# Who makes the rests of the weights: GpSimd or VectorE, and how many tiles are made ahead

## The chip, the cores and the metric

The kernel runs on one core of a Trainium2 chip. The time is device microseconds (us) of one execution; the median of three runs of the kernel before is 943.08 us (942.50 to 943.26). Lower is better.

## The reference

Windowed attention, then an MLP with the maximum of three products, then a gated MLP, all in float32:

```python
scores = 1/sqrt(64) * q @ k.T + bias          # 4 batches, 8 heads, 576 tokens, 64 deep
attn   = softmax(where((0 <= i - j) & (i - j < 128), scores, -1e9))
x      = (attn @ v)                           # 2304 tokens x 512
h      = maximum(maximum(x @ w1, x @ w2), x @ w3)      # w: 512 x 768
x      = h @ w_out                                      # 768 x 512
g      = x @ w_gate; val = x @ w_val                    # 512 x 1536
out    = (g * sigmoid(g) * val) @ w_out2                # 1536 x 512
```

The weights of both MLPs are float64 in memory.

## The kernel before

TensorE multiplies float32 here as three products of a narrower format: an operand is split into its rounding (the head) and what is left (the rest), and head x head + head x rest + rest x head is summed in PSUM (`mm3`). So every operand needs a rounding and a subtraction, `low`, which makes the rest.

A weight tile (128 rows x 512 columns) comes from memory as pairs of 32-bit words. `prep_w` makes a float32 of it and splits it: ScalarE scales the upper word (L93), VectorE does three bit steps (L94, L95, L97), ScalarE rounds to the head (L100), and GpSimd subtracts the head, which is the rest (L80, called at L101). In the rows these are `wf` (the work tile, two places), `wr` (the raw words) and `w`, `wo` or `u` (the made tile of the first MLP's up or down weights, or of the second MLP).

The first MLP runs per sub-chunk of a batch, 256 or 320 tokens, eight in all, with the attention of the sub-chunks to come between its products; its 18 up tiles and 6 down tiles (in 12 halves) are made while the first sub-chunks run. For each 128 features VectorE takes the maximum of three products (L155), and GpSimd rounds and splits it (`h`). The result y goes to memory.

The second MLP runs over all 2304 tokens in chunks of 512 (the last has 256), with its 36 tiles resident: for each of 12 blocks f of 128 features the gate's, the value's and the output's. `gate(c, f)` multiplies y by two tiles (24 products), ScalarE takes the sigmoid (L503), VectorE multiplies twice (L504, L505), GpSimd rounds (L83) and splits (L80) the result `a`; `down(c, t, f)` adds it to the output sums of 128 tokens (3 products each). A gate stands ahead of the down products of the block before it. `load_y(0)` loads and splits the four pieces of y of the first chunk through the two `wf` places. Raw words of the second MLP have four places (`RAWS`).

C2 and C3 say how many of the 36 tiles are made at which point: `conv[:C2]` are spread among the last sub-chunk's up products (and the down products ahead of them), `conv[C2:C3]` with `load_y(0)` among its last down products, three more ahead of gate(0, 0), and then three for each block of chunk 0. The order of the instructions of each engine is set from this program order by a scheduler that models the engines' times; each engine then runs its own list strictly in order. All loads and stores are issued by SyncE (SP), also in order.

Of the kernel before, what the change touches and what calls it, by code (L numbers as in the profile page):

```python
# [30 lines left out]
FILL = -float(2.0 ** 100)  # L31
# places for the second MLP's words to arrive
RAWS = 4
NATIVE = 12, 10
C0, C1, C2, C3 = 0, 0, 6, 9
HIGH, EARLY = 100, 3
# [11 lines left out]
LN, LT, LV = 1, 2, 4  # L48
# the upper word of a float64 of 2**-127, read as a float32
LEAST = 1.0 * 2.0 ** -15  # L50
# [3 lines left out]
def kernel(ctx: ExitStack, tc, qk0, qk1, vv, w123, wo1, wgv, wo2, out):  # L54
    """Windowed attention, then max-of-three MLP, then gated MLP, all in float32.

    Products of float32 operands run as three float32r passes: an operand is split exactly into a
    12-bit head (its rounding to float32r) and the 12-bit rest, and head*head + head*rest +
    rest*head is summed in PSUM. Weights come as the words of float64 and become float32 here.

    The first MLP runs per sub-chunk of a batch (256 and 320 tokens), with the attention of the
    sub-chunks to come between its products; the second runs over all tokens with its weights
    resident, in chunks of 512.
    """
    nc = tc.nc
# [18 lines left out]

    # -------- weights: [P, head/rest, 512] tiles
    def prep_w(raw, t):
        """float64 words to float32 to head and rest. The bits: sign and top exponent bit, the
        exponent's low seven bits and the mantissa's first twenty, then its next three; under
        2**-126 it becomes 0."""
        n = raw.shape[1]  # L90
        lo, hi = raw[:, :, 0], raw[:, :, 1]
        w = wraw.tile([P, 512], I32, tag="wf", name="wf")[:, :n]
        nc.scalar.activation(out=w.bitcast(F32), in_=hi.bitcast(F32), func=AF.Copy, scale=2.0 ** -112)  # L93
        nc.vector.tensor_scalar(out=w, in0=w, scalar1=3, scalar2=None, op0=ALU.logical_shift_left)  # L94
        nc.vector.scalar_tensor_tensor(out=w, in0=hi, scalar=-0x80000000, in1=w,  # L95
                                       op0=ALU.bitwise_and, op1=ALU.bitwise_or)
        nc.vector.scalar_tensor_tensor(out=lo, in0=lo, scalar=29, in1=w,  # L97
                                       op0=ALU.logical_shift_right, op1=ALU.bitwise_or)
        lo = lo.bitcast(F32)
        nc.scalar.copy(t[:, 0], lo)  # L100
        low(nc.gpsimd, t[:, 1], lo, t[:, 0])  # L101

# [6 lines left out]
    def mm3(ps, wt, col, xt_h, xt_l, first, last):  # L109
        """ps += w.T @ x over one 128-deep slice, w's columns col..col+128."""  # L110
        wh, wl = wt[:, 0, col:col + P], wt[:, 1, col:col + P]
        nc.tensor.matmul(ps, wh, xt_h, start=first, stop=False)  # L112
        nc.tensor.matmul(ps, wh, xt_l, start=False, stop=False)  # L113
        nc.tensor.matmul(ps, wl, xt_h, start=False, stop=last)  # L114

    # -------- first MLP
    x_t, w1, wo, hs = {}, {}, {}, {}
# [9 lines left out]
    def prep_up(f, e):  # L127
        if (f, e) not in w1:
            load_up(f, e)
        raw, w1[f, e] = w1[f, e], up_tile(f"w1_{f}_{e}")  # L130
        prep_w(raw, w1[f, e])

    def prep_down(k):
        wo[k] = down_tile(f"wo_{k}")
        for i in range(2):
            src = wo1[k * P:(k + 1) * P, i * 256:i * 256 + 256]
            raw = words(src, wraw, "wr", 256) if i else words(src, tmp, "y", 256)
            prep_w(raw, wo[k][:, :, i * 256:i * 256 + 256])

    def up_groups(b, s):  # L140
        """The up products of a sub-chunk, three experts per 128 features."""
        n = SUBS[s][1]
# [21 lines left out]
    def down_groups(b, s):  # L164
# [8 lines left out]
        def group(ds):  # L173
            # the last features of two columns after the others of both
            ps = [ps_m.tile([P, 512], F32, tag="m", name="ps2") for d in ds]
# [28 lines left out]

    # -------- attention pieces
    def load_pair(b, s, p):
# [30 lines left out]
    def native(b, s, p, i):  # L237
        """Whether the scores (0) or the values (1) are multiplied in float32 itself, which takes
        the tensor engine longer and the others less: at the start, while it has no other work."""
        return SKIP[i] <= todo.index((b, s, p)) < NATIVE[i]  # L240
# [18 lines left out]
    class Unit:  # L259
        """A pair of heads and a block of 128 queries, against the block's keys and those before."""  # L260

# [9 lines left out]
    def st_scores(u):  # L271
# [5 lines left out]
        for a in range(2):  # L277
# [8 lines left out]
            nc.tensor.matmul(o, q, kl[:, c0 - nq:c1 - nq], start=False, stop=True)  # L286
        # query q sees key k of its own block for k <= q, of the block before for k > q: one square
        own = sc[:m, :, P:]
# [30 lines left out]
    def st_transpose(u):  # L319
        """The weights with keys in front, head and rest, of the block before and of the own block."""  # L320
        m = u.mq
# [75 lines left out]

    # attention in the order of its pieces: a unit's later pieces come after the next units' first
    units = [Unit(b, s, p, j) for b, s in order for p in range(NP) for j in BLOCKS[s]]
# [45 lines left out]
    def spread(main, *others, early=0):  # L445
        """Calls main's pieces in turn, with each other list's spread evenly in front of all but
        the last few."""
        done = [0] * len(others)
        for i, g in enumerate(main):
            for n, o in enumerate(others):  # L450
                while done[n] < len(o) and done[n] * (len(main) - early) <= i * len(o):
                    o[done[n]]()
                    done[n] += 1
            g()
        for n, o in enumerate(others):
            for piece in o[done[n]:]:
                piece()

    # -------- second MLP
    w2 = {}  # L460

    def second(w2pool, raws2, ps_o):
        y_t, acts, ps = {}, {}, {}

        def prep(f, i):
# [6 lines left out]
            src = wgv[f, :, i] if i < 2 else wo2[f * P:(f + 1) * P]  # L472
            prep_w(words(src, raws2, "wr2", 512), t)

# [16 lines left out]
        def gate(c, f):  # L491
            """128 features of the gated product."""
            n = CHUNKS[c][1]
# [18 lines left out]
        def down(c, t, f):  # L512
            """What those features give 128 tokens."""
            if f == 0:
# [13 lines left out]

    # the tensor engine's clock rises after some microseconds of work
    cold = tmp.tile([P, 512], BF16, tag="m0", name="cold")  # L530
# [36 lines left out]

    # the products of a feature block go into the outputs of the whole chunk while the next
    # block's run; the first chunk goes over each weight as it comes
    spread([lambda: gate(0, 0)], conv[C3:C3 + 3])  # L570
# [53 lines left out]
```

## Time and profile before

| | |
|---|---|
| median of three runs | 943.08 us |
| span of the profiled execution | 939.2 us (some 3.9 us lie around it) |
| TensorE (PE) busy | 904.2 us, 96% of the span |
| VectorE (DVE) busy | 497.4 us, 53% |
| GpSimd (POOL) busy | 472.4 us, 50% |
| ScalarE (ACT) busy | 354.2 us, 38% |
| chain that ended last | PE 76%, DVE 11%, issue 4%, POOL 4%, DMA 4% |

Shares of the whole span hide the stages: the attention and the first up products to about 125 us, the rest of the first MLP to 463 us, the first chunk of the second MLP with the making of its weights to 560 us, and four more chunks to 935 us. "PEclk" in a row is the mean clock that TensorE was granted in that stretch, as a share of full speed (1.0 is 2.4 GHz, 0.5 is 1.2 GHz).

### The profile page before, as it was taken

The numbers are of one execution on the slowest core, as the hardware profiler recorded it, in microseconds if no ns is written. First come the engines' busy times: TensorE is split into PE (matmuls) and PEld (weight loads), VectorE is DVE, ScalarE is ACT, GpSimd is POOL, SyncE is SP. The second block draws the span as 40 slices with busy tenths as digits, with TensorE's granted clock in tenths as the row PEclk, the third lists the DMA queues.
The fourth block names the chain that finished last, engine by engine and source line by source line (L and its number), as shares of the span: only waits on it lengthen the run. The fifth ranks groups of instructions, "written<-read, shape, count | busy, mean of one in ns | idle before, by whom it ended". The sixth has DMA issues, their size and how long they took to land.

```text
span 939.2 us, 14970 instructions
## 1 busy us (share of the span) xinstructions
PE 904.2 (96%) x5268; PEld 791.3 (84%) x5268; DVE 497.4 (53%) x1295; ACT 354.2 (38%) x974; POOL 472.4 (50%) x655
## 2 busy tenths in 40 slices
PE   8899999999999999999997789999999999999998
PEld 5577789999999999999975568888888888888897
DVE  4699987767677676637799983211121112111121
ACT  3576756856576656513444431200020002000101
POOL 3599997676767766545566652222222222222222
PEclk9998999999999999999998999999999999999999
DMA  9743242314121331004544431200020001000100
GB/s 211 256 147 107 73 131 82 97 57 145 59 86 52 116 94 34 9 23 167 196 159 138 154 122 30 73 1 1 1 79 0 1 1 57 1 1 0 45 1 23
DMA packets 34187, 71.10 MB, mean 76 GB/s; under 512 B 3648, under 2 KB 13120, under 8 KB 34112
## 3 DMA queue, kind: packets, MB, share of 16 engines
q1 hardware_dynamic: 34112, 70.14, 23.3%
q8 instruction: 42, 0.69, 0.3%
q14 instruction: 33, 0.27, 0.1%
HBM read 60.69 MB, written 9.44 MB: 75 GB/s over the span
## 4 chain that ended last, share of the span: by engine, by line
PE 76%; DVE 11%; issue 4%; POOL 4%; DMA 4%; ACT 1%; SPq 0%; ACTq 0%; DVEq 0%; POOLq 0%
PE ps L113 9%; PE ps L114 9%; PE ps L112 9%; PE pg L112 9%; PE pg L113 9%; PE pg L114 9%; PE po L520 5%; PE po L518 5%; PE po L519 5%; DVE wf L95 4%; DVE wr L97 3%; PE pv L369 2%; DVE wf L94 2%; PE pt L326 2%; PE sc L281 1%
## 5 line engine op out<-in xcount | busy, mean ns | idle before, releaser
L83 POOL TENSOR_SCALAR a<-sg 128x512 fp32r<-128x512 f32 (+1 forms) x60 | 36.3, 605 | 286.4 <-DVE sg L505 283.0
L112 PE MATMUL pg<-y,u 128*128 128x512 f32 (+1 forms) x480 | 177.0, 369 | 0.0
L113 PE MATMUL pg<-y,u 128*128 128x512 f32 (+1 forms) x480 | 176.8, 368 | 0.0
L114 PE MATMUL pg<-y,u 128*128 128x512 f32 (+1 forms) x480 | 176.8, 368 | 0.0
L113 PE MATMUL ps<-x,w 128*128 128x320 f32 (+1 forms) x576 | 175.5, 306 | 1.0 <-POOL x L80 1.0
L112 PE MATMUL ps<-x,w 128*128 128x320 f32 (+1 forms) x576 | 173.4, 305 | 2.0 <-DVE m L155 2.0
L114 PE MATMUL ps<-x,w 128*128 128x320 f32 (+1 forms) x576 | 174.2, 303 | 0.0
L504 DVE TENSOR_TENSOR sg<-pg,sg 128x512 f32<-128x512 f32 (+1 forms) x60 | 38.2, 636 | 233.3 <-ACT sg L503 233.3
L503 ACT ACTIVATE sg<-pg 128x512 f32<-128x512 f32 (+1 forms) x60 | 33.2, 554 | 296.5 <-PE pg L114 292.1
L113 PEld LDWEIGHTS ps<-x,w 128*128 128x128 f32 x576 | 111.1, 193 | 4.7 <-issue 2.5
L112 PEld LDWEIGHTS ps<-x,w 128*128 128x128 f32 x576 | 109.6, 192 | 5.9 <-DVE m L155 2.5
L114 PEld LDWEIGHTS ps<-x,w 128*128 128x128 f32 x576 | 110.9, 193 | 1.9 <-issue 1.2
L112 PEld LDWEIGHTS pg<-y,u 128*128 128x128 f32 x480 | 90.8, 189 | 15.5
L113 PEld LDWEIGHTS pg<-y,u 128*128 128x128 f32 x480 | 90.8, 189 | 15.5
L114 PEld LDWEIGHTS pg<-y,u 128*128 128x128 f32 x480 | 90.6, 189 | 15.2
L518 PE MATMUL po<-u,a 128*128 128x512 f32 x216 | 86.8, 402 | 9.6 <-POOL a L83 9.5
L520 PE MATMUL po<-u,a 128*128 128x512 f32 x216 | 87.1, 405 | 8.4 <-POOL a L80 8.3
L342 POOL TENSOR_SCALAR_AFFINE_SELECT t<-pk 128x512 fp32r<-128x512 f32 (+3 forms) x128 | 74.6, 605 | 36.4 <-PE pv L369 21.3
L519 PE MATMUL po<-u,a 128*128 128x512 f32 x216 | 86.0, 398 | 0.0
L80 POOL TENSOR_TENSOR u<-wr,u 128x512 fp32r<-128x512 f32 x36 | 56.3, 1570 | 38.5 <-ACT u L100 38.4
L80 POOL TENSOR_TENSOR a<-sg,a 128x512 fp32r<-128x512 f32 (+1 forms) x60 | 71.8, 1197 | 4.8
L299 ACT ACTIVATE z<-z,mn 128x128 f32<-128x128 f32 (+1 forms) x160 | 63.1, 396 | 20.5 <-DVE mn L294 20.1
(84 smaller groups left out, 1771.8 us busy)
## 6 DMA issues: line engine op xcount, KB each, us to landing
wr<-wgv SPq DMA_DIRECT2D x24, 512.0 KB, 3.5
qkr<-qk SPq DMA_DIRECT2D x24, 416.0 KB, 3.6
wr<-w SPq DMA_DIRECT2D x18, 512.0 KB, 4.5
wr<-wo SPq DMA_DIRECT2D x12, 512.0 KB, 3.5
out<-ob SPq DMA_DIRECT2D x18, 256.0 KB, 2.0
qkr<-qk SPq DMA_DIRECT2D x16, 256.0 KB, 2.8
yraw<-y_dram SPq DMA_DIRECT2D x16, 256.0 KB, 2.8
wr<-wo SPq DMA_DIRECT2D x12, 256.0 KB, 3.1
```

The lines of the kernel that those rows point to most:

```text
L80: eng.tensor_tensor(out=out, in0=raw, in1=head.bitcast(F32), op=ALU.subtract)
L83: nc.gpsimd.tensor_scalar(out=out, in0=in_, scalar1=1.0, scalar2=1.0, op0=ALU.mult, op1=ALU.mult)
L95: nc.vector.scalar_tensor_tensor(out=w, in0=hi, scalar=-0x80000000, in1=w, op0=ALU.bitwise_and, op1=ALU.bitwise_or)
L112: nc.tensor.matmul(ps, wh, xt_h, start=first, stop=False)
L113: nc.tensor.matmul(ps, wh, xt_l, start=False, stop=False)
L114: nc.tensor.matmul(ps, wl, xt_h, start=False, stop=last)
L299: nc.scalar.activation(out=z[:m, a], in_=z[:m, a], func=AF.Exp, scale=-1.0, bias=mn[:m, a:a + 1], accum_out=sm[:m, a:a + 1],)
L342: nc.gpsimd.affine_select(out=t[:, i, :n, :, :m], in_=w[:, :n, :, :m], compare_op=op, fill=0.0, base=0, pattern=[[0, n], [0, 2], [-sign, m ...
L504: nc.vector.tensor_tensor(out=sg, in0=pair[0], in1=sg, op=ALU.mult)
L518: nc.tensor.matmul(po, ah, w2[f, 2][:, 0, :], start=f == 0, stop=False)
L519: nc.tensor.matmul(po, ah, w2[f, 2][:, 1, :], start=False, stop=False)
L520: nc.tensor.matmul(po, al, w2[f, 2][:, 0, :], start=False, stop=f == NF2 - 1)
```

## The change

`prep_w` gets the engine that makes the rest as an argument, and all three callers, for the up and the down tiles of the first MLP and for the second MLP's, give VectorE. So 66 subtractions (54 of 512 columns, 12 of 256) go from GpSimd's list to VectorE's. C2 and C3 go from 6 and 9 to 12 and 15. Comments and docstrings go too.

```diff
-C0, C1, C2, C3 = 0, 0, 6, 9
+C0, C1, C2, C3 = 0, 0, 12, 15
...
-    def prep_w(raw, t):
+    def prep_w(raw, t, eng):
...
-        low(nc.gpsimd, t[:, 1], lo, t[:, 0])
+        low(eng, t[:, 1], lo, t[:, 0])
...
-        prep_w(raw, w1[f, e])
+        prep_w(raw, w1[f, e], nc.vector)
...
-            prep_w(raw, wo[k][:, :, i * 256:i * 256 + 256])
+            prep_w(raw, wo[k][:, :, i * 256:i * 256 + 256], nc.vector)
...
-            prep_w(words(src, raws2, "wr2", 512), t)
+            prep_w(words(src, raws2, "wr2", 512), t, nc.vector)
```

**VectorE in chunk 0.** VectorE's list from the fifth gate's first product (L504) on; `sg` is the gate's product, `wf_...` and `wr_...` the steps of one weight tile. Before:

```order
L504 TENSOR_TENSOR sg_7272<-pg_7246,sg_7272 128x512
L94 TENSOR_SCALAR wf_7305<-wf_7305 128x512
L95 SCALAR_TENSOR_TENSOR wf_7305<-wr_7303,wf_7305 128x512
L505 TENSOR_TENSOR sg_7272<-pg_7259,sg_7272 128x512
L97 SCALAR_TENSOR_TENSOR wr_7303<-wr_7303,wf_7305 128x512
L94 TENSOR_SCALAR wf_7315<-wf_7315 128x512
L95 SCALAR_TENSOR_TENSOR wf_7315<-wr_7313,wf_7315 128x512
L97 SCALAR_TENSOR_TENSOR wr_7313<-wr_7313,wf_7315 128x512
```

The same place of the changed kernel, from the fifth gate's first product on (`u_22` to `u_24` are weight tiles 22 to 24):

```order
L504 TENSOR_TENSOR sg_7332<-pg_7306,sg_7332 128x512
L94 TENSOR_SCALAR wf_7147<-wf_7147 128x512
L80 TENSOR_TENSOR u_22_7134<-wr_7135,u_22_7134 128x512
L505 TENSOR_TENSOR sg_7332<-pg_7319,sg_7332 128x512
L94 TENSOR_SCALAR wf_7203<-wf_7203 128x512
L95 SCALAR_TENSOR_TENSOR wf_7147<-wr_7145,wf_7147 128x512
L95 SCALAR_TENSOR_TENSOR wf_7203<-wr_7201,wf_7203 128x512
L97 SCALAR_TENSOR_TENSOR wr_7145<-wr_7145,wf_7147 128x512
L97 SCALAR_TENSOR_TENSOR wr_7201<-wr_7201,wf_7203 128x512
L80 TENSOR_TENSOR u_23_7144<-wr_7145,u_23_7144 128x512
L94 TENSOR_SCALAR wf_7213<-wf_7213 128x512
L80 TENSOR_TENSOR u_24_7200<-wr_7201,u_24_7200 128x512
```

The rests stand on VectorE, mostly with steps of the next tile between L97 and the rest; the fifth gate comes at tile 22 or 23, and before at tile 25.

**SP at the end of the first MLP.** SP's list around the loads of the first chunk's y (`yraw`); `wr` are words of weight tiles. Before, from the words of tile 6 (`wr_6847`) on:

```order
L121 DMA wr_6847<-wgv 128x1024
L487 DMA yraw_6786<-y_dram_78 128x512
L121 DMA wr_6879<-wgv 128x1024
L121 DMA wr_6911<-wo2 128x1024
L487 DMA yraw_6790<-y_dram_78 128x512
L487 DMA yraw_6794<-y_dram_78 128x512
L121 DMA wr_6921<-wgv 128x1024
L487 DMA yraw_6798<-y_dram_78 128x512
```

Of the changed kernel, from the words of tile 12 (`wr_6907`) on:

```order
L121 DMA wr_6907<-wgv 128x1024
L487 DMA yraw_6846<-y_dram_78 128x512
L121 DMA wr_6939<-wgv 128x1024
L183 DMA y_dram_78<-y_6897 128x320
L183 DMA y_dram_78<-y_6903 128x320
L121 DMA wr_6971<-wo2 128x1024
L487 DMA yraw_6850<-y_dram_78 128x512
L487 DMA yraw_6854<-y_dram_78 128x512
L183 DMA y_dram_78<-y_6935 128x320
L121 DMA wr_6981<-wgv 128x1024
L183 DMA y_dram_78<-y_6967 128x320
L487 DMA yraw_6858<-y_dram_78 128x512
```

The first load of y stands behind the words of 13 tiles instead of 7, and the others among the stores of the last down products (L183).

**TensorE at the start of the second MLP.** TensorE's list from gate(0, 0)'s first product on; `pg` are the sums of a gate's two halves, `u_0`, `u_1`, `u_3`, `u_4` the tiles of blocks 0 and 1. Before:

```order
L112 MATMUL pg_6930<-y_6784,u_0_6360 128x512
L113 MATMUL pg_6930<-y_6784,u_0_6360 128x512
L114 MATMUL pg_6930<-y_6784,u_0_6360 128x512
L112 MATMUL pg_6930<-y_6784,u_0_6360 128x512
L113 MATMUL pg_6930<-y_6784,u_0_6360 128x512
L114 MATMUL pg_6930<-y_6784,u_0_6360 128x512
L112 MATMUL pg_6930<-y_6785,u_0_6360 128x512
```

Of the changed kernel:

```order
L112 MATMUL pg_6990<-y_6844,u_0_6360 128x512
L112 MATMUL pg_7003<-y_6844,u_1_6436 128x512
L113 MATMUL pg_6990<-y_6844,u_0_6360 128x512
L114 MATMUL pg_6990<-y_6844,u_0_6360 128x512
L113 MATMUL pg_7003<-y_6844,u_1_6436 128x512
L114 MATMUL pg_7003<-y_6844,u_1_6436 128x512
L112 MATMUL pg_7074<-y_6844,u_3_6524 128x512
L113 MATMUL pg_7074<-y_6844,u_3_6524 128x512
```

All four sums of the first two gates are now built side by side, slice of y by slice of y.

## Rows read from the trace of the kernel before

**Rows 1.** Stages: start:end us, length, each engine's busy time, PEclk, DMA

```profile
48.00:85.00 37.00, 34.11 (x245) 26.31 (x243) 35.64 (x108) 28.40 (x89) 36.66 (x46) 1.00 0.49 153
85.00:125.00 40.00, 38.75 (x242) 31.43 (x241) 38.48 (x100) 27.11 (x82) 37.32 (x54) 0.87 0.29 92
125.00:424.00 299.00, 299.00 (x2300) 294.71 (x2300) 199.22 (x717) 175.30 (x559) 204.44 (x346) 1.00 0.23 72
424.00:463.50 39.50, 37.52 (x254) 36.98 (x253) 31.04 (x43) 16.87 (x31) 22.83 (x20) 1.00 0.51 179
475.00:552.00 77.00, 60.58 (x226) 45.23 (x225) 74.92 (x80) 30.37 (x51) 48.92 (x37) 0.91 0.42 144
560.50:935.00 374.50, 374.45 (x1786) 315.42 (x1785) 74.26 (x119) 45.13 (x83) 89.89 (x104) 1.00 0.06 20
```

In these rows the engines stand as PE, PEld (weight loads), DVE, ACT, POOL, each with its number of instructions.

**Rows 2.** Chain that ended last, 551 to 561 us: start, us, engine, tile, line

```profile
551.23 0.70 DVE wr L97
...
560.25 0.50 PE po L520
```

**Rows 3.** TensorE's instructions in time: start, us, line, out<-in, shape, count

```profile
463.66 0.39 PE L112 MATMUL pg<-y,u 128*128 128x512 f32 x1
...
759.65 0.39 PE L114 MATMUL pg<-y,u 128*128 128x512 f32 x1
...
766.68 0.39 PE L112 MATMUL pg<-y,u 128*128 128x512 f32 x1
...
890.80 0.28 PE L112 MATMUL pg<-y,u 128*128 128x256 f32 x1
...
893.55 0.28 PE L114 MATMUL pg<-y,u 128*128 128x256 f32 x1
...
934.33 0.62 PE L520 MATMUL po<-u,a 128*128 128x512 f32 x2
```

**Rows 4.** VectorE's instructions in time, 500 to 506 us

```profile
500.13 1.53 DVE L94 TENSOR_SCALAR wf<-wf 128x512 int32<-128x512 int32 x1
...
503.49 0.69 DVE L97 SCALAR_TENSOR_TENSOR wr<-wr,wf 128x512 int32<-128x512 int32 x1
504.10 0.42 DVE L94 TENSOR_SCALAR wf<-wf 128x512 int32<-128x512 int32 x1
504.43 0.68 DVE L504 TENSOR_TENSOR sg<-pg,sg 128x512 f32<-128x512 f32 x1
505.03 1.78 DVE L95 SCALAR_TENSOR_TENSOR wf<-wr,wf 128x512 int32<-128x512 int32 x1
```

**Rows 5.** GpSimd's instructions in time, the same stretch, with idle time before

```profile
499.59 3.24 POOL L80 TENSOR_TENSOR u<-wr,u 128x512 fp32r<-128x512 f32 x2 [1.66 <-ACT u L100]
504.95 1.31 POOL L80 TENSOR_TENSOR u<-wr,u 128x512 fp32r<-128x512 f32 x1 [2.12 <-ACT u L100]
```

**Rows 6.** Groups in 475 to 552: count | busy us, mean ns | idle before

```profile
L80 POOL TENSOR_TENSOR u<-wr,u 128x512 fp32r<-128x512 f32 x23 | 35.7, 1560 | 22.4 <-ACT u L100 22.4
...
L94 DVE TENSOR_SCALAR wf<-wf 128x512 int32<-128x512 int32 x23 | 20.3, 883 | 0.0
...
L504 DVE TENSOR_TENSOR sg<-pg,sg 128x512 f32<-128x512 f32 x6 | 4.1, 681 | 0.0
```

**Rows 7.** Groups in 600 to 900 us, where no weights are made

```profile
L80 POOL TENSOR_TENSOR a<-sg,a 128x512 fp32r<-128x512 f32 x35 | 45.0, 1286 | 2.9
L83 POOL TENSOR_SCALAR a<-sg 128x512 fp32r<-128x512 f32 x35 | 21.7, 620 | 216.0 <-DVE sg L505 216.0
...
L80 DVE TENSOR_TENSOR y<-yraw,y 128x512 fp32r<-128x512 f32 x4 | 2.7, 692 | 2.0 <-ACT y L488 2.0
```

**Rows 8.** y's loads (count, KB, us to landing); the first L504

```profile
yraw<-y_dram SPq DMA_DIRECT2D x16, 256.0 KB, 2.8
...
472.16 0.68 DVE L504 TENSOR_TENSOR sg<-pg,sg 128x512 f32<-128x512 f32 x1
```

**Rows 9.** GpSimd's rests of up tiles as a group, 48 to 125 us

```profile
L80 POOL TENSOR_TENSOR w<-wr,w 128x512 fp32r<-128x512 f32 x14 | 20.0, 1427 | 0.0
```

## The prediction

> **What bounds the kernel now.** I read first the busy time by stage [rows 1], then where the chain of waits turns from one engine to another [rows 2], then single instructions. From 125 to 424 us TensorE is busy in all 299.00 us, and from 560.5 to 935 in 374.45 of 374.50: there only TensorE's own work counts. Elsewhere it waits. In 48 to 125 it is idle for 2.9 + 1.25 us, and its granted clock is 0.87 in the second half; in 475 to 552 it is busy for 60.58 of 77 us at a granted clock of 0.91. In these stretches VectorE is busy for 96 to 97% of the time [rows 1], and the chain runs through it: at 551.23 it does the last L97, the last bit step of the last weight tile, and at 560.25 TensorE goes on and waits no more [rows 2].
>
> How much is lost there? The first product of the second MLP starts at 463.66 and the last ends at 934.33 + 0.62 = 934.95, so it takes 471.3 us [rows 3]. Undisturbed, 512 columns take (766.68 - 759.65) / 31 = 0.2268 us and 256 columns (893.55 - 890.80) / 23 = 0.1196 us [rows 3]. Four chunks of 12 x 36 products and 72 of the last chunk are 1800 x 0.2268 = 408.2, and 288 x 0.1196 = 34.4: together 442.7 us. So **28.6 us are lost**, all of them in chunk 0, while its weights are made.
>
> What makes VectorE slow there? The same L94 takes 0.42 us at 504.10 and 1.53 at 500.13; the L95 at 505.03 takes 1.78 [rows 4]. The long ones lie beside GpSimd's rests (499.59 to 502.83, 504.95 to 506.26 [rows 5]), and the L95 ends at 506.81, a short one's length after the rest; at 504.10 GpSimd is idle. So they wait for GpSimd, and "97% busy" is mostly waiting. The Trainium skill, "SBUF — State Buffer", section "Who interferes with whom", has this as a rule: a VectorE instruction with two SBUF inputs, or in a two-port mode, and a GpSimd instruction exclude each other, and the later one waits for the whole of the earlier. The trace agrees, with 0.42 against 1.53 us; by the rule in full the ratio that I find next would be 1 instead of 0.80, and the sum below 3 us worse.
>
> The price from this stage: VectorE's 80 instructions in 475 to 552 [rows 1] are 23 L94, 45 of L95 and L97, and 12 of the gate (six L504, six L505) [rows 6]. Without waiting they follow each other after 0.33 (504.10 to 504.43), 0.61 (503.49 to 504.10) and 0.60 us (504.43 to 505.03) [rows 4]: 7.6 + 27.5 + 7.2 = 42.3 us. The other 34.7 are waits. GpSimd's 37 instructions [rows 1] are 23 rests of weights [rows 6] and 14 of the gate, 7 roundings and 7 rests; undisturbed 1.31 [rows 5], 1.29 and 0.62 [rows 7]: 43.4 us. So VectorE pays **0.80 us for each us of GpSimd's work**.
>
> **The change, step by step.** (1) *36 rests of the second MLP on VectorE.* None stands in the trace. The nearest row is the same operation on y, 512 columns, both inputs in SBUF: 0.692 us busy on VectorE with GpSimd mostly idle [rows 7]; L97, which reads the same strided words, takes 0.69 [rows 4]. I take 0.61 from one to the next. The lower end is the same; the upper is 1.78 [rows 4], were it to wait as L95 does, but that wait is priced below. The rest adds a wait of VectorE for ScalarE's cast (L100); behind it stand the next tile's steps and the gate products, for which GpSimd's rounding and TensorE wait. The order puts steps of the next tile between L97 and the rest, so I count nothing for it here. A tile then costs 0.33 + 3 x 0.61 = 2.16 us instead of 1.55, and GpSimd's 1.31 x 0.80 = 1.05 of waiting goes: 0.44 less per tile.
>
> (2) *The order.* Between the gate products VectorE has fewer tiles: from the first L504 to the ninth L505 of chunk 0 the changed order has 21 L94, 62 of L95, L97 and rests, and 18 gate products. In the kernel before, the last tile was done around the eighth gate; now it is after the ninth. So 6.9 + 37.8 + 10.8 = 55.5 us, and the GpSimd work that is left beside it, 8 x (0.62 + 1.29) x 0.80 = 12.2: **67.7 us for eight gates, 8.5 each; TensorE needs 36 x 0.2268 = 8.16.** In 475 to 552 six gates went by, 12.8 us each. TensorE stays held up, but barely.
>
> (3) *The start.* Before, the first L504 was at 472.16 [rows 8]. Now 13 tiles stand ahead of it with 13 x 0.61 = 7.9 us more of VectorE and up to 12 x 1.05 = 12.6 us of waits less. But SP issues the four loads of y behind the words of tiles 12 to 14, which wait for the rests of tiles 8 to 10, and y has two places, so the loads go in two rounds of 2.8 us [rows 8] with a cast and a rest each. The changed order does two gates slice by slice as y arrives, which covers part of it. Bounds: 0 (y needed no sooner than TensorE is free) and +12 us; I take +6.5, nearer to the upper end as two rounds with cast and rest are some 8 us: the first L504 at 478.7.
>
> (4) *The sum of chunk 0.* The ninth L505 ends at 478.7 + 67.7 = 546.4; with the rounding and half of the gate's rest TensorE starts that gate's down products at 547.7. Undisturbed it would be there at 463.66 + 10 x 24 x 0.2268 + 8 x 12 x 0.2268 = 539.9. So it lags by 7.8 us, and from then on nothing of weights holds it. The tail of the first MLP (424 to 463.5, TensorE busy 37.52 of 39.50 [rows 1]) gets maxima that queue behind rests on VectorE: 0 to 4 us, I take 1.5; and 1 for gaps between dependent instructions. 28.6 - 7.8 - 2.5 = **18.3 us gained**, with ends of 7 (start +12, ratio 1, tail 4) and 27 (start 0).
>
> (5) *The first MLP, 18 + 12 rests.* In 48 to 125 GpSimd loses 14 tiles of 1.43 us [rows 9] and the halves of the down weights; VectorE gets 14 x 0.61 = 8.5 and loses 14 x 1.31 x 0.80 = 14.7 of waits. Both are relieved. But TensorE can win no more than its idle 4.1 us and what the lower clock took: 0.13 of 40 us of granted clock is 5.2 us. From 125 on TensorE hides everything. Ends: -8.5 (the rests add and no wait goes) and +9.3; I take **+2**, as the waits of TensorE here are on attention steps of several engines.
>
> Sum 20.3; the span was 939.2 and the median of the runs 943.1, the 3.9 around the span stay: **923 us**.
>
> **Rivals.** *TensorE never waits* (chance 0.15): the waits shrink more than in proportion, y comes in time. Then 28.6 - 2.5 + 4 = 30 us less: 913. For it: 8.5 is already near 8.16. Against: y's loads are queued behind more tiles.
>
> *Half of it* (0.16): each pair of GpSimd's instructions costs VectorE its full length (+3), the gates start at +10 instead of +6.5, gaps cost 3 more, and the first MLP gives nothing: 20.3 - 3 - 3.5 - 3 - 2 = 9 us less, 934.
>
> *VectorE is the bound by its own work* (0.06): if the 1.53 and 1.78 are what strided words cost, nothing goes away, and each rest adds about 1 us to an engine that is 97% busy. The 23 tiles of 475 to 552 then take 23 us more: 943 + 23 = 966. It decides from a gate's 8.5 becoming 8.5 + 18.3 / 8 = 10.8 us. Against it stand the short instructions of the same form [rows 4]. The Trainium skill, "Perfetto Trace Analysis", section "Optimizing Scalar/DVE Operations", speaks against the change in the same sense: from a saturated VectorE work may go to GpSimd; it adds that this might not help, as the two share a read port.
>
> *It does what it says and nothing comes of it* (0.03): y so late that TensorE stands still for 18 us more at 464: 943. That the rests move is plain from the order.
>
> **How the numbers follow.** The forecast has 0.60. 912 to 936 holds nearly all of it, half of the first rival and most of the second, about 0.8. Faster is the forecast and the first two rivals, 0.91; same 0.03; slower 0.06. What a measurement of this kernel can tell from no change is about 0.2%, some 2 us.
>
> **What would show it.** Right: L94 near 0.42 and L95, L97 and the new rests near 0.69 in 475 to 552; gates 8 to 10 us apart; TensorE's idle time there cut from 16.4 to under 8 us; the stretch to 125 us shorter by a little. Wrong: L95 still over 1 us with GpSimd idle; TensorE idle for over 10 us ahead of the first gate product; or lost time in 125 to 424, which the reordered instructions could bring though no row hints at it.

## The result, and the profile after

| | before | after |
|---|---|---|
| median of the runs | 943.17 us (942.50 to 943.44) | 918.92 us (914.77 to 922.02) |
| ratio, 95% interval | | 0.9732 (0.9694 to 0.9770) |
| span of the profiled execution | 939.2 us | 916.0 us (a run of 917.72) |
| first load of the second MLP's words issued | 423.71 | 420.03 |
| first product of the second MLP | 463.66 | 459.39 |
| its last product ends | 934.95 | 911.74 |
| so the second MLP takes | 471.3 us | 452.35 us |
| of it lost (442.7 us are needed) | 28.6 us | 9.7 us |

The changed kernel is 2.7% faster. Of the 23.2 us of the span, 3.7 came before 424 us, 0.6 in the tail of the first MLP (from those loads to the first product: 39.95 us before, 39.36 now) and 18.9 in chunk 0.

The busy shares of the page after (busy us, share of the span, instructions): GpSimd has lost 69 us against 472.4, but VectorE, which got the 66 rests, is at 486.2 us, *less* than the 497.4 before.

```profile
PE 891.2 (97%) x5268; PEld 785.1 (86%) x5268; DVE 486.2 (53%) x1361; ACT 353.8 (39%) x974; POOL 403.9 (44%) x589
```

The windows by stage, in the columns of [rows 1], with the bounds moved to where the stages now lie:

```profile
48.00:85.00 37.00, 36.52 (x264) 27.64 (x263) 35.07 (x126) 29.81 (x102) 29.27 (x47) 1.00 0.47 147
85.00:125.00 40.00, 38.01 (x258) 32.66 (x259) 38.26 (x112) 28.28 (x83) 29.63 (x44) 0.91 0.28 85
...
420.30:460.00 39.70, 38.02 (x258) 37.67 (x257) 35.09 (x61) 18.63 (x33) 17.97 (x12) 1.00 0.61 203
...
471.30:548.00 76.70, 71.56 (x309) 57.26 (x308) 73.75 (x112) 35.04 (x59) 29.99 (x18) 1.00 0.44 148
...
556.80:912.00 355.20, 354.94 (x1701) 299.35 (x1699) 68.59 (x110) 42.82 (x78) 84.34 (x98) 1.00 0.05 18
```

In 471 to 548 VectorE is as full as before, but does 112 instructions where it did 80 in the same time [rows 1]; TensorE's idle time there falls from 16.4 to 5.1 us and its granted clock stands at 1.00 instead of 0.91 (0.09 of 77 us is 6.9 us). The groups (count | busy us, mean ns | idle before) answer [rows 6]. Before, in 475 to 552 us:

```profile
L95 DVE SCALAR_TENSOR_TENSOR wf<-wr,wf 128x512 int32<-128x512 int32 x22 | 27.8, 1262 | 0.4
...
L83 POOL TENSOR_SCALAR a<-sg 128x512 fp32r<-128x512 f32 x7 | 6.1, 867 | 6.9 <-DVE sg L505 6.9
```

After, in 470 to 545 us:

```profile
L80 DVE TENSOR_TENSOR u<-wr,u 128x512 fp32r<-128x512 f32 x23 | 19.8, 861 | 0.3 <-ACT u L100 0.2
L95 DVE SCALAR_TENSOR_TENSOR wf<-wr,wf 128x512 int32<-128x512 int32 x23 | 18.4, 811 | 0.0
...
L94 DVE TENSOR_SCALAR wf<-wf 128x512 int32<-128x512 int32 x23 | 12.1, 527 | 0.2 <-ACT wf L93 0.2
...
L83 POOL TENSOR_SCALAR a<-sg 128x512 fp32r<-128x512 f32 x9 | 16.7, 1855 | 60.2 <-DVE sg L505 60.2
```

L94 takes 527 ns instead of 883, L95 811 instead of 1262. But look at the last line: GpSimd's rounding of the gate, which takes 620 ns alone [rows 7] and took 867 here before, now takes 1855 in the mean. Three of the nine make that mean (4.67, 3.14 and 3.14 us); the other six take 0.72 to 1.06. The longest of them, on GpSimd (first two lines), on VectorE beside it, and on TensorE, which waits for it (in brackets the idle time before, and its releaser):

```profile
495.53 4.67 POOL L83 TENSOR_SCALAR a<-sg 128x512 fp32r<-128x512 f32 x1 [8.38 <-DVE sg L505]
500.28 1.59 POOL L80 TENSOR_TENSOR a<-sg,a 128x512 fp32r<-128x512 f32 x1
```

```profile
495.96 0.68 DVE L80 TENSOR_TENSOR u<-wr,u 128x512 fp32r<-128x512 f32 x1
496.56 0.42 DVE L94 TENSOR_SCALAR wf<-wf 128x512 int32<-128x512 int32 x1
496.90 0.68 DVE L80 TENSOR_TENSOR u<-wr,u 128x512 fp32r<-128x512 f32 x1
...
499.04 0.68 DVE L95 SCALAR_TENSOR_TENSOR wf<-wr,wf 128x512 int32<-128x512 int32 x1
499.75 0.98 DVE L97 SCALAR_TENSOR_TENSOR wr<-wr,wf 128x512 int32<-128x512 int32 x1
500.66 1.76 DVE L80 TENSOR_TENSOR u<-wr,u 128x512 fp32r<-128x512 f32 x1
```

```profile
500.25 0.50 PE L518 MATMUL po<-u,a 128*128 128x512 f32 x1 [1.10 <-POOL a L83]
...
501.93 0.51 PE L520 MATMUL po<-u,a 128*128 128x512 f32 x1 [0.94 <-POOL a L80]
```

So part of the wait has changed sides. Before, VectorE's steps waited for GpSimd's rests. In these rows VectorE runs one instruction after another, 0.60 us apart, and the rounding that came at 495.53 ends only at 500.2, while seven of VectorE's begin and end in between. Then GpSimd's rest of the gate stretches a rest on VectorE to 1.76 us, as the old ones did. The waits of TensorE in 455 to 560 us (engine, tile, line waited for: total, times, longest) that such roundings and rests end are these; before, in 455 to 565, they were 8.3 and 9.5 us:

```profile
PE po L520 <- POOL a L80: 2.5, 3, 0.9
...
PE po L518 <- POOL a L83: 1.1, 1, 1.1
```

### The profile page after: what moved, and what is told of

Read it like the earlier page. It is cut to its first block, busy times and chain, and to the rows that moved or that the text cites. A ratio compares the mean times of both kernels' runs of the same rounds, so it can differ in the third digit from the quotient of the medians.

```text
span 916.0 us, 14901 instructions
## 1 busy us (share of the span) xinstructions
PE 891.2 (97%) x5268; PEld 785.1 (86%) x5268; DVE 486.2 (53%) x1361; ACT 353.8 (39%) x974; POOL 403.9 (44%) x589
## 4 chain that ended last, share of the span: by engine, by line
PE 77%; issue 8%; POOL 5%; DVE 5%; DMA 3%; ACT 1%; SPq 0%; ACTq 0%; POOLq 0%; DVEq 0%
PE ps L112 9%; PE pg L113 9%; PE pg L114 9%; PE pg L112 9%; PE ps L113 9%; PE ps L114 9%; PE po L520 5%; PE po L519 5%; PE po L518 5%; PE pv L369 3%; PE pt L326 2%; PE sc L281 2%; POOL a L83 2%; DMA qkn<-qk 2%; PE sc L285 1%
## 5 line engine op out<-in xcount | busy, mean ns | idle before, releaser
L83 POOL TENSOR_SCALAR a<-sg 128x512 fp32r<-128x512 f32 (+1 forms) x60 | 45.8, 763 | 334.9 <-DVE sg L505 331.5
L112 PE MATMUL ps<-x,w 128*128 128x256 f32 (+1 forms) x576 | 174.2, 305 | 0.9 <-DVE m L155 0.4
L113 PE MATMUL ps<-x,w 128*128 128x320 f32 (+1 forms) x576 | 173.9, 303 | 0.0
L114 PE MATMUL ps<-x,w 128*128 128x320 f32 (+1 forms) x576 | 173.6, 302 | 0.1
L504 DVE TENSOR_TENSOR sg<-pg,sg 128x512 f32<-128x512 f32 (+1 forms) x60 | 38.2, 636 | 227.9 <-ACT sg L503 227.9
L520 PE MATMUL po<-u,a 128*128 128x512 f32 x216 | 83.9, 391 | 2.5 <-POOL a L80 2.5
L518 PE MATMUL po<-u,a 128*128 128x512 f32 x216 | 84.5, 391 | 1.1 <-POOL a L83 1.1
L519 PE MATMUL po<-u,a 128*128 128x512 f32 x216 | 84.2, 390 | 0.0
L80 POOL TENSOR_TENSOR a<-sg,a 128x512 fp32r<-128x512 f32 (+1 forms) x60 | 72.4, 1207 | 5.0
L505 DVE TENSOR_TENSOR sg<-pg,sg 128x512 f32<-128x512 f32 (+1 forms) x60 | 38.1, 636 | 52.0 <-PE pg L114 51.7
```

The costliest lines, as they stand in the source:

```text
L80: eng.tensor_tensor(out=out, in0=raw, in1=head.bitcast(F32), op=ALU.subtract)
L83: nc.gpsimd.tensor_scalar(out=out, in0=in_, scalar1=1.0, scalar2=1.0, op0=ALU.mult, op1=ALU.mult)
L504: nc.vector.tensor_tensor(out=sg, in0=pair[0], in1=sg, op=ALU.mult)
L505: nc.vector.tensor_tensor(out=sg, in0=pair[1], in1=sg, op=ALU.mult)
L518: nc.tensor.matmul(po, ah, w2[f, 2][:, 0, :], start=f == 0, stop=False)
L519: nc.tensor.matmul(po, ah, w2[f, 2][:, 1, :], start=False, stop=False)
```

## Experiments

In every trace the same three places were read: the first load of wgv (the end of what the first MLP does alone), the first product `pg`, and the end of the last `po`. "Lost" is the time between the last two less 442.7 us.

| | rests on | C2, C3 | median us | ratio to before (95%) | load | load to product | lost |
|---|---|---|---|---|---|---|---|
| before | GpSimd | 6, 9 | 943.17 | | 423.7 | 39.9 | 28.6 |
| after | VectorE | 12, 15 | 918.92 | 0.9732 (0.9694 to 0.9770) | 420.0 | 39.4 | 9.7 |
| e1_engine_alone | VectorE | 6, 9 | 916.27 | 0.9701 (0.9670 to 0.9732) | 418.8 | 37.4 | 10.7 |
| e2_order_alone | GpSimd | 12, 15 | 951.08 | 1.0069 (1.0035 to 1.0104) | 425.6 | 48.0 | 28.8 |
| e3_second_only | first GpSimd, second VectorE | 12, 15 | 926.81 | 0.9807 (0.9767 to 0.9847) | 425.2 | 39.5 | 12.5 |
| e4_first_only | first VectorE, second GpSimd | 6, 9 | 938.40 | 0.9929 (0.9902 to 0.9955) | 420.4 | 40.3 | 29.5 |
| e5_pool_idle_work | VectorE | 6, 9 | 947.60 | 1.0033 (1.0014 to 1.0052) | 417.7 | 53.5 | 28.6 |
| e6_no_rest | nobody (second) | 6, 9 | 911.35 | 0.9650 (0.9629 to 0.9671) | 419.2 | 37.4 | 5.4 |
| e7_gate_off_pool | VectorE | 6, 9 | 905.18 | 0.9604 (0.9575 to 0.9633) | 424.1 | 37.4 | 0.3 |
| e8_gate_round_act | VectorE | 6, 9 | 914.65 | 0.9676 (0.9646 to 0.9707) | 424.8 | 37.4 | 5.2 |
| e9_gate_off_pool_order | VectorE | 12, 15 | 910.79 | 0.9651 (0.9613 to 0.9689) | 420.2 | 41.0 | 1.5 |
| e10_after_again | VectorE | 12, 15 | 919.73 | 0.9739 (0.9708 to 0.9771) | 419.1 | 41.2 | 8.3 |
| e11_warm | VectorE | 6, 9 | 899.88 | 0.9529 (0.9504 to 0.9554) | 417.6 | 37.4 | 0.3 |
| e12_again | VectorE | 6, 9 | 905.65 | 0.9592 (0.9565 to 0.9620) | 418.5 | 38.1 | 1.1 |

### Which part of the change: the engine or the order

The engine alone, with the old C2 and C3 (of the changed kernel):

```diff
-C0, C1, C2, C3 = 0, 0, 12, 15
+C0, C1, C2, C3 = 0, 0, 6, 9
```

> The changed kernel, but with the order of the kernel before (C2, C3 = 6, 9 instead of 12, 15). Theory 1 (GpSimd's rests of weights kept VectorE waiting; the order matters little): most of the 24 us stay, 919 to 927 us; chunk 0 loses 10 to 16 us instead of 28.6, L95 and L97 there near 0.8 us. Theory 2 (the order brings the gain: more tiles are done when the first gate starts): 937 to 944 us.

Measured: 916.27 us (915.59 to 917.18), 2.7 us below what theory 1 expected: all of the gain, and 2.7 us more, which is within the scatter of the changed kernel's runs. Chunk 0 loses 10.7 us, with L95 and L97 at 0.75 and 0.89 us in the mean of 470 to 545. The order alone (of the kernel before):

```diff
-C0, C1, C2, C3 = 0, 0, 6, 9
+C0, C1, C2, C3 = 0, 0, 12, 15
```

> The kernel before with C2, C3 = 12, 15 alone; the rests stay on GpSimd. Theory 1: VectorE has the same work and the same waits, only more of it ahead of the first gate, so TensorE waits earlier instead of later: 937 to 948 us, the first L504 later than 472.16 us. Theory 2: 919 to 930 us.

Measured: 951.08 us, slower by 0.7%, 3 us beyond the end of what was expected, and the first L504 at 486.53. TensorE's waits from 417 to 478 us say where; before, the view of 410 to 466 us has 2.0 us, for L155 alone:

```profile
PE ps L112 <- DVE m L155: 4.0, 4, 1.3
PE ps L112 <- POOL h L83: 2.9, 1, 2.9
PE pg L112 <- ACT y L488: 0.7, 1, 0.7
```

Six more tiles ahead of the first gate stand among the last maxima of the first MLP (L155), and the way from the loads to the first product takes 48.0 us instead of 39.9. (In 48 to 60 us this run does 46 products where the trace before has 82, the late change of level of which more below; but its load comes only 1.9 us later.) Chunk 0 gains nothing from it: it loses 28.8 us, as before. So theory 1 holds, and the order is a cost of 0.7% (interval 1.0035 to 1.0104).

### Which MLP

```diff
-        prep_w(raw, w1[f, e], nc.vector)
+        prep_w(raw, w1[f, e], nc.gpsimd)
...
-            prep_w(raw, wo[k][:, :, i * 256:i * 256 + 256], nc.vector)
+            prep_w(raw, wo[k][:, :, i * 256:i * 256 + 256], nc.gpsimd)
```

> The changed kernel, but the rests of the first MLP's up and down tiles stay on GpSimd. Theory 1 with the prediction's split (chunk 0 gains 18 to 19 us, the first MLP 4): the second MLP starts as late as before (first load of its words issued near 423.7 us) and the total is 921 to 925 us. Rival (what the first MLP gains is due to the order, or to nothing): the same time as the changed kernel, 917 to 921 us.

Measured: 926.81 us (922.59 to 929.10), 8 us above the changed kernel where 2 to 6 were expected: the load comes 5.1 us later, and chunk 0 lost 2.8 us more. VectorE's instructions there are as short as the changed kernel's (L95 811 ns, L94 518 in 475 to 550 us), but TensorE's granted clock was 0.89 in 505 to 520 and in 535 to 550 us, right after waits of 2.0 and 3.3 us, and 1.00 in every 15 us of chunk 0 in the changed kernel's trace; 0.11 of 30 us is 3.3 us. That fits the size; no run separates it. The other half, of the first experiment:

```diff
-            prep_w(words(src, raws2, "wr2", 512), t, nc.vector)
+            prep_w(words(src, raws2, "wr2", 512), t, nc.gpsimd)
```

> The kernel before, but with the rests of the first MLP's tiles on VectorE; those of the second stay on GpSimd, C2, C3 = 6, 9. Theory 1: only the 4 us of the first MLP, 937 to 941 us; the second MLP still loses about 28 us. Rival (the early relief of GpSimd brings most of it): under 932 us.

Measured: 938.40 us. The first MLP's rests bring some 5 us, the second MLP's the rest (e4 to e1: 22 us).

### Does GpSimd's work hold VectorE, or the chain through it?

The first experiment, with work on GpSimd that nobody waits for:

```diff
-        low(eng, t[:, 1], lo, t[:, 0])
+        low(eng, t[:, 1], lo, t[:, 0]); extra and low(nc.gpsimd, tmp.tile([P, 512], F32, tag="y", name="nobody"), t[:, 0].bitcast(F32), t[:, 0])
```

> The first experiment (rests on VectorE, C2, C3 = 6, 9; 916 us, gates of chunk 0 9.13 us apart), to which GpSimd gets back one subtraction per tile of the second MLP: of the finished head from itself, into a tile that nobody reads. VectorE has the same list; nothing waits for the new instruction. Theory 1 (GpSimd's instructions keep VectorE's waiting, whoever needs their result): 3 x 1.31 x 0.80 = 3.1 us more per gate, gates near 12.2 us, L95 and L97 in chunk 0 over 1.0 us again, 934 to 945 us. Theory 2 (it was the chain through GpSimd that held the tiles up, a rest awaited, a buffer held): 915 to 920 us, the mean of L95 and L97 unchanged.

Measured: 947.60 us (944.24 to 949.32), 2.6 us above the range of theory 1 and 0.3% above the kernel before, and **chunk 0 loses 28.6 us again**. From the second L504 (485.85) to the ninth (568.72) the gates are 11.84 us apart instead of 9.13 (471.80 to 535.68 in e1). `nobody` stands ahead of gate work in GpSimd's list, so a gate could also wait there; but VectorE is busy in all but 0.21 of 80 us, so it sets the pace:

```profile
485.00:565.00 80.00, 65.89 (x250) 49.92 (x250) 79.79 (x97) 27.60 (x47) 44.95 (x35) 0.91 0.41 137
```

VectorE, and GpSimd in the same time:

```profile
501.81 1.09 DVE L95 SCALAR_TENSOR_TENSOR wf<-wr,wf 128x512 int32<-128x512 int32 x1
502.93 1.64 DVE L97 SCALAR_TENSOR_TENSOR wr<-wr,wf 128x512 int32<-128x512 int32 x1
504.50 1.53 DVE L80 TENSOR_TENSOR u<-wr,u 128x512 fp32r<-128x512 f32 x1
505.95 1.26 DVE L94 TENSOR_SCALAR wf<-wf 128x512 int32<-128x512 int32 x1
507.13 0.68 DVE L80 TENSOR_TENSOR u<-wr,u 128x512 fp32r<-128x512 f32 x1
```

```profile
502.44 1.58 POOL L80 TENSOR_TENSOR a<-sg,a 128x512 fp32r<-128x512 f32 x1
503.99 2.93 POOL L80 TENSOR_TENSOR nobody<-u 128x512 f32<-128x512 f32 x2
```

VectorE's steps beside them last about as long as those of GpSimd; at 507.13, when GpSimd is idle, the same rest takes 0.68. That is the exclusion by itself. The new work costs 2.71 us per gate for 3 x 1.31 = 3.93 us of GpSimd's, 0.69 for each. That the loss is the same 28.6 us as before is chance: VectorE has the rests besides. (The means of L95 and L97 in 470 to 545 rose only to 0.88 and 0.95 us where over 1.0 was expected; the waits fell more on L94, 0.46 to 0.88, and on the rests, 0.86 to 1.14. And part of the time is my choice of the place for `nobody`: it shares the places of the first MLP's y, and TensorE waited once for the copy of y (L182), 10.6 us. That is most of the 16.1 us by which the 53.5 in the table is above e1's 37.4. Without these the kernel would be at some 931 to 937 us, an estimate that takes off 16.1 or 10.6.)

### What still holds chunk 0: VectorE's rests, or GpSimd's gate work

No rests at all in the second MLP:

```diff
-        low(eng, t[:, 1], lo, t[:, 0])
+        eng and low(eng, t[:, 1], lo, t[:, 0])
...
-            prep_w(words(src, raws2, "wr2", 512), t, nc.vector)
+            prep_w(words(src, raws2, "wr2", 512), t, None)
```

> The first experiment without any rest of the second MLP's weights: none is made, and TensorE reads the head in its place. What VectorE pays for the rests now: 3 x 0.61 = 1.8 us per gate. Theory 1 (VectorE's own work is what holds the gates at 9.13 us): 9.13 - 1.8 = 7.3, below TensorE's 8.16, so TensorE hardly waits and the total is 904 to 910 us. Theory 2 (something else, such as the round of gate and down products, holds the gates at 9.13): 914 to 918 us.

Measured: 911.35 us, above the 904 to 910 of theory 1 and below theory 2. Chunk 0 still loses 5.4 us without a rest on VectorE, which is then busy in only 58.12 of 75 us (470 to 545). So without VectorE's rests half of the 10.7 us of the first experiment goes. What TensorE still waits for in 455 to 565 us is GpSimd's two instructions per gate:

```profile
PE po L520 <- POOL a L80: 2.9, 5, 0.9
```

These two instructions are now taken from GpSimd, while VectorE keeps the rests of the weights:

```diff
-                pool_round(ah, sg)
-                low(nc.gpsimd, al, sg, ah)
+                nc.scalar.copy(ah, sg)
+                low(nc.vector, al, sg, ah)
```

> The first experiment, with the gate's rounding on ScalarE and its rest on VectorE, so that GpSimd has nothing to do in the second MLP. Theory (the roundings now wait for gaps of VectorE, up to 4.67 us in the changed kernel, and TensorE waits 7.7 us for them in the first experiment): VectorE loses 1.5 us of waits per gate and gets 0.6 of work, gates near 8.2 us, TensorE's waits for GpSimd gone, 906 to 911 us. Rival (the wait only changes its name, VectorE's own queue delays the gate's rest as long): 914 to 919 us.

Measured: 905.18 us (904.66 to 910.49), 0.8 us below the range of the theory and some 1% below the first experiment (0.9604 and 0.9701 of the kernel before). Windows of this kernel, in the columns of [rows 1], and groups of 470 to 545 us:

```profile
470.00:545.00 75.00, 75.00 (x332) 62.03 (x331) 72.84 (x131) 43.47 (x73) 0.00 (x0) 1.00 0.52 169
461.50:904.50 443.00, 443.00 (x2090) 372.17 (x2088) 181.42 (x307) 119.92 (x210) 0.00 (x0) 1.00 0.15 50
```

```profile
L80 DVE TENSOR_TENSOR u<-wr,u 128x512 fp32r<-128x512 f32 x26 | 17.8, 685 | 0.0
L97 DVE SCALAR_TENSOR_TENSOR wr<-wr,wf 128x512 int32<-128x512 int32 x25 | 17.1, 686 | 0.1
...
L94 DVE TENSOR_SCALAR wf<-wf 128x512 int32<-128x512 int32 x24 | 10.1, 421 | 0.0
L80 DVE TENSOR_TENSOR a<-sg,a 128x512 fp32r<-128x512 f32 x10 | 6.9, 685 | 0.0
```

With GpSimd at 0.00, each of VectorE's means is the undisturbed one, VectorE does 131 instructions in 75 us, and TensorE is busy in all 443.00 us of the second MLP: 0.3 us are lost. That beats the kernel in which nobody makes the rests. So the two halves do not add: the gate's two instructions leaving GpSimd is worth 10.4 of the 10.7 us by itself, with the rests still on VectorE. Half a step, the rounding alone on ScalarE:

```diff
-                pool_round(ah, sg)
+                nc.scalar.copy(ah, sg)
```

> As the seventh experiment, but only the gate's rounding goes to ScalarE; its rest stays on GpSimd. Theory: one of the two waits of TensorE for GpSimd goes (3.9 of 7.7 us), and 0.62 x 0.80 = 0.5 us of VectorE's waits per gate: 909 to 913 us, between the first and the seventh experiment. Rival: 914 to 919 us, as the rest on GpSimd starves alone.

Measured: 914.65 us (911.23 to 917.49), a miss: it lies in the rival's range. Chunk 0 loses 5.2 us, halfway as expected, but the traced run's load came at 424.8, 6 us later than the first experiment's: in 48 to 60 us TensorE does 56 products in it and 89 in e1, the late change of its clock level that is shown below. The rest on GpSimd takes 2.10 us in the mean of 470 to 545, and L97 0.99, which is what the rival said of it.

The same two edits as in the seventh experiment, with C2, C3 = 12, 15:

> The changed kernel (C2, C3 = 12, 15) with the gate's rounding on ScalarE and its rest on VectorE, as in the seventh experiment (905 us with C2, C3 = 6, 9). Theory (tiles made before the first gate only make it later; they help no more once VectorE keeps up): the tail of the first MLP and the way to the first gate stay 2 to 4 us longer, 906 to 910 us. Rival (the order pays when VectorE is relieved, as the tiles are then made in time): 901 to 905 us.

Measured: 910.79 us, 0.8 above the range of the theory and 5.6 above the seventh experiment; load to product 41.0 us instead of 37.4. In all three pairs (e2 and before, after and e1, e9 and e7) the larger C2 and C3 have the higher median, by 7, 2.7 and 5.6 us; the second difference is within the scatter of the runs. In the traces the way from the load to the first product is longer by 8.0, 1.9 and 3.6 us.

### The scatter, and the time before 165 us

The changed kernel once more, unchanged:

> The changed kernel once more, for a second trace of it: its runs lie 7 us apart, those of the kernel before 1 us. Theory (the spread comes ahead of 165 us, from how long TensorE's first products run at half speed): 914 to 922 us, the second MLP again 452 to 453 us from its first product to its last, and the first y stored earlier or later by what the time differs. Rival (chunk 0 itself scatters): the second MLP differs from 452.35 us by over 2 us.

Measured: 919.73 us (917.30 to 923.57). Its second MLP took 451.04 us, 1.3 from the first trace's. But both traces are of runs near 917.5, so neither shows what a run of 922 does, and the scatter of this kernel stays open. The seventh experiment again, where two groups of runs had shown:

> The seventh experiment once more, for a trace of the faster of its two groups of runs (its trace was of a run of 910.5 us, with long products until 52.4 us and 443.0 us from the first to the last product of the second MLP). Theory: a run of 905 us has the short products 8 to 10 us earlier and the same 443 us. Rival: the second MLP takes 5 us less in it, which the columns forbid, or the first MLP differs elsewhere.

Measured: 905.65 us (905.49 to 908.02); the traced run was the one of 908.0. The traces of e7 and of this run are of the same program and do the same work to 43.5 us. Windows of the run of 910.5 us, and one of its products of 128x256:

```profile
40.00:44.00 4.00, 4.00 (x16) 2.98 (x14) 2.25 (x10) 1.09 (x6) 3.44 (x7) 1.00 0.47 147
44.00:52.00 8.00, 8.00 (x29) 4.87 (x27) 3.70 (x17) 3.44 (x11) 1.98 (x5) 1.00 0.32 98
...
55.07 0.41 PE L114 MATMUL ps<-x,w 128*128 128x256 f32 x1
```

and of the run of 908.0 us:

```profile
40.00:44.00 4.00, 4.00 (x16) 2.92 (x14) 2.23 (x10) 1.12 (x6) 3.41 (x7) 1.00 0.46 138
44.00:52.00 8.00, 8.00 (x56) 5.62 (x56) 7.20 (x28) 6.57 (x23) 4.47 (x9) 1.00 0.34 98
...
43.57 0.40 PE L113 MATMUL ps<-x,w 128*128 128x256 f32 x1
...
46.21 0.28 PE L113 MATMUL ps<-x,w 128*128 128x256 f32 x1
```

TensorE is busy in both throughout, and does 29 products in one and 56 in the other. Right behind another product of its shape, one of 128x256 lasts 0.41 us at the lower of TensorE's two levels (1.2 GHz; two of them begin 0.21 us apart) and 0.28 at the higher (0.12 apart). In the one trace the long ones go on to 55.07, in the other they end at 43.57: TensorE stays at the lower level for at least 11.5 us longer. The 0.58 us of the next expectation is only that of the first of a row of such products, so the 52.4 us of the one above is too early an end of the long ones. The first load of wgv comes 5.6 us later in the first trace. The second MLP took 443.0 and 443.8 us: the theory's side, though the faster group of 905.5 itself has no trace. Then, to end the lower level sooner:

```diff
-WARM, WN = 24, 256
+WARM, WN = 56, 256
```

> The seventh experiment (runs at 905 and 910 us) with 56 instead of 24 of the products of zeros that keep TensorE busy ahead of its first work (L532 to L534); the scheduler puts them into its idle places of the first 30 us. Theory (products of 128x256 last 0.58 us until 42 to 57 us and 0.28 us after, and the early change of that costs or gives 3 to 5 us): with TensorE busy all along the short ones begin before 42 us, and the time is 898 to 905 us, without a second group at 910. Rival (the moment doesn't depend on idle time at the start): 904 to 911 us, as before.

Measured: 899.88 us (898.32 to 903.94), the fastest here, 4.7% below the kernel before. The time is the theory's, its reason isn't: TensorE was busy in 20 to 48 us with 0.5 us of idle time (before the edit 4.2), yet products of 0.41 us still come until 43.63, no earlier than in e12 (43.57). The load of wgv comes 0.9 us earlier than there. The trace is of the run of 903.9, the slowest of the six, so where the others gain stays open.

## Why the prediction was right, step by step

The forecast was 923 us, with 912 to 936 around it; 918.92 was measured.

- *What bounds.* Right, and shown by itself: GpSimd's work without any reader brings the whole 28.6 us back (e5). The 0.80 us that VectorE pays per us of GpSimd's was 0.69 there. In e1 a gate takes 9.13 us, of which 3 x 2.16 + 1.2 = 7.68 are VectorE's own, so 1.45 for 1.91 us of GpSimd's: 0.76. The 0.80 was a little high by its own rows: of the 34.7 us called waits, 77 - 74.92 = 2.1 are idle time [rows 1], which leaves 0.75.
- *Step 1, the rests at 0.61.* Right: 0.60 from one to the next in the trace after, 0.685 busy where GpSimd is idle (e7).
- *Step 2, 67.7 us for eight gates.* Right: from the first L504 to the end of the ninth L505 it is 473.65 to 540.90, 67.25 us:

```profile
473.65 0.68 DVE L504 TENSOR_TENSOR sg<-pg,sg 128x512 f32<-128x512 f32 x1
...
540.22 0.68 DVE L505 TENSOR_TENSOR sg<-pg,sg 128x512 f32<-128x512 f32 x1
```

- *Step 3, the start at 478.7.* As a distance right: 15.0 us after the first product were expected, and it was 14.26 (459.39 to 473.65). As the step has it, y came in parts (its casts begin at 457.77, 462.98 and, the last, 469.15) and the gates built side by side covered most of that: TensorE waited 1.7 us for the casts (L488) and 1.5 for the first L504. The absolute time fell with the first product, which came 4.3 us earlier.
- *Step 4, 18.3 us from chunk 0 and the tail.* Chunk 0 gave 18.9 where 19.8 were expected (28.6 - 7.8 - 1). What I had not in the sum is the starved rounding on GpSimd: the 3.6 us that TensorE waits for L83 and L80 all stand behind the three long roundings. Only e7 showed what GpSimd's gate work is worth in all, together with its cost on VectorE. The tail, put at -1.5, was +0.6. The sign was wrong for this reason: the rests on VectorE alone shorten it by 2.5 us (e1: 37.4), and the order takes 2 to 4 back (39.4 and 41.2 in the two traces of the changed kernel).
- *Step 5, the first MLP, +2.* Mis-sized: 3.7 us in the trace; e4, with only these rests moved, has its load at 420.4, 3.3 us earlier, and is 0.7% faster. VectorE's means in 48 to 125 us fell as the step says (L95 899 to 712 ns, L97 974 to 746). Both of the step's bounds gave something: TensorE's idle time in 48 to 125 us fell from 4.1 to 2.5 us, and its granted clock in 85 to 125 rose from 0.87 to 0.91, 0.04 of 40 us, which is 1.6 us. That is 3.3 of the 3.7. None of it came earlier: TensorE had done 223 products by 60 us where the kernel before had done 226, and 660 by 125 us where that had done 629.
- *The order as such* is the step that the working lacks. C2 and C3 were priced only inside steps 2 and 3, never alone; alone they cost 7 us (e2), 5.6 with the gate off GpSimd (e9), and with the change itself 2.7, which its scatter does not tell from nothing. The "fewer tiles between the gates" of step 2 is true but was paid for ahead of the first gate, where the same VectorE makes the same tiles between maxima that TensorE waits for.
- *Rivals.* "TensorE never waits" didn't come with this change; with C2 and C3 as before it needed only the gate's two instructions to leave GpSimd (e7). "VectorE is the bound by its own work" is refuted by L94 at 0.42 and L95 at 0.68 us wherever GpSimd is idle, on the same strided words; of the two pages of the Trainium skill that I weighed, "Perfetto Trace Analysis", section "Optimizing Scalar/DVE Operations", has its caveat borne out here, not its advice: 916.27 us with 66 subtractions moved from GpSimd onto VectorE (e1), 0.9701 of the kernel before.

In the sum: 1.7 us more from the first MLP, 2.1 more in the tail and 0.9 less in chunk 0 make the 2.9 us by which the span fell more than forecast. The median lies 3.9 us below the unrounded 922.8. The other 1.0 is there because the "3.9 us around the span" did not stay: in the runs that have both on record, time and span differ by 1.7 to 3.2 us, mostly 1.7 (here 917.72 and 916.0, with the median 1.2 above this run). The trace of the kernel before, of 939.2 us, is of a shorter execution than all its runs with a span on record (940.0 to 948.3), so differences of spans to it come out some 2 us too small.

## What to carry to other kernels

Where VectorE is "97% busy" and the same instruction takes 0.42 and 1.53 us, look at what GpSimd does beside the long one before moving more work to GpSimd: here taking work *from* it onto the full engine freed VectorE. Two engines that exclude each other are to be counted almost as one (0.69 to 0.80 us for each us here), and what must be prompt (here the gate's rounding, for which TensorE waits) should be on neither of them while the other is full, but on ScalarE. Work made ahead cost time here, because its engine held somebody up where it was made; test such a number apart from the change that it comes with.

## What the runs showed of the hardware

- Who waits is not only a matter of who came first. The Trainium skill, "SBUF — State Buffer", section "Who interferes with whom", says that the one that issues first has the ports for its whole instruction and the order decides who blocks. Of the nine roundings in 470 to 545 us of the changed kernel's trace, six agree: the next instruction of VectorE is the longer one, and the rounding ends in 0.72 to 1.06 us. Three don't. With VectorE's instructions 0.60 us apart or less, a rounding of 0.62 us on GpSimd took 4.67 us, by its recorded start and end, and instructions of VectorE that began after it went ahead. In the rows above it ends 0.45 us after the first place where two of VectorE's begin 0.71 us apart instead of 0.60 (499.04 and 499.75, an L95 and the L97 that needs it); the other two, of 3.14 us, end 0.46 and 0.33 us after steps of 0.71 and 0.84. That these three slip into such a gap is my reading, not shown by a run of its own, and the six needed no gap. What decides between them is not shown.
- TensorE's granted clock stood at 1.00 in the windows of 44 to 52 us of both runs of one program, while it did 29 products in one and 56 in the other. In the first 60 us the clock's level is read from the duration of one shape, not from that column. The two runs did the same up to 43.5 us, and the lower level ended at least 11.5 us apart (products of 0.41 us until 43.57 and until 55.07).
